# Output projection of two token blocks: seven half-size products for eight, with stored weight sums

## The chip, the core and the metric

The kernel runs on one core of a Trainium2 chip. The core has a matrix engine (TensorE: PE, with its weight loads PEld), a vector engine (DVE), a scalar engine (ACT), a general engine (POOL), and SyncE (SP), which here issues nearly all DMA transfers. The metric is the device time of one execution in microseconds; the time before is the median of three.

## The reference

Two independent branches are computed and laid side by side. Branch A is an attention with 32 heads that share one key and one value head. Branch B is a real part of a two-dimensional Fourier transform, written as products with given matrices.

```python
# A: x (2048 x 1024), wq (1024 x 1024), wk, wv (1024 x 32), wo (1024 x 1024)
q = (x @ wq).reshape(B, S, 32, 32).transpose(0, 2, 1, 3)
k = x @ wk
v = x @ wv
p = softmax(einsum("bhqd,bkd->bhqk", q, k) * 32 ** -0.5)
o = einsum("bhqk,bkd->bhqd", p, v)
out_a = o.transpose(0, 2, 1, 3).reshape(B, S, 1024) @ wo
# B: x (2048 x 1024), four transform matrices
a = einsum("bsd,ed->bse", x, hid_re); b = einsum("bsd,ed->bse", x, hid_im)
out_b = einsum("ts,bse->bte", seq_re, a) - einsum("ts,bse->bte", seq_im, b)
concatenate([out_a, out_b], axis=-1)
```

The change touches the last line of A, `o @ wo`: 2048 tokens by 1024 by 1024.

## The kernel before

**Arithmetic.** Inputs are 32-bit floats. For the projections and for branch B each operand is split into a high part, a cast to `F32R`, and a low part, what is left of it. A product of two operands is three matmuls: high x high, low x high, high x low (`product`). Each is 128 x 128 by 128 x 512. POOL casts the high part (`hi_r`, `hi_m`) and subtracts for the low part (`lo`); where an operand is a sum of blocks, POOL adds first (`comb`).

**Two streams on TensorE.** One is the attention, cut into 32 units (4 blocks of 512 tokens by 8 groups of 4 heads). A unit is 32 steps; a step has two score matmuls for row maxima and row sums of a later unit (`scores`, tiles `pss`, then a row maximum on DVE and an exponential on ACT), two score matmuls that give exponentials (`expo`, tiles `pst`), and every 8th step 32 small products with the values (`pv`, 128 x 32 weights, tiles `psb`). The main loop has 1024 steps; the row sums run 44 steps ahead (`SU + LEAD`) and so end at step 980.

The other stream is a list of groups that holds everything else: the query projection (positions 0 to 768 of the list), the first stage of branch B (768 to 2112), its second stage (2112 to 4800), then the output projection of the blocks 0 to 2 (`o_group`, 4800 to 5376). Eight more groups, the output projection of block 3, are added shortly before the end and run behind the loop, with the attention's last piece. A position is one matmul; `pos["fill"]` is where the list stands. `goal` and `level` spread the list over the steps: 404 positions lie ahead of the loop, then (5376 - 404 - 24 - 44) / 1024 = 4.789 a step, and one more a step from step 980 on. TensorE executes exactly this interleaving.

**Sevenfold products.** Both stages of branch B already go by seven half-size products in place of eight (`STAGE1`, `PRODUCTS`): sums of blocks are multiplied, and results are added up in partial sums kept in DRAM. In the first stage a group is 12 matmuls; its fifth product (name `p5`, positions 1536 to 1728) loads two partial sums for every group (`y`), adds TensorE's result on DVE and stores both.

**Output projection.** The attention's result for a unit is scaled, cast and subtracted on POOL (`ends`), and its two parts go to DRAM (`oh_d`, `ol_d`). `o_group` takes 128 tokens and 512 output columns: 8 inner blocks x 3 = 24 matmuls, one copy out of the accumulator on DVE, one store. The left parts are loaded ready split, two transfers of 256 KB for four inner blocks; `wo` is loaded and split on the way (`wo_set`, 8 tiles for 512 columns).

**What sets the order.** The program is written out by hand in order, engine by engine (`Ordered`); each engine executes its instructions strictly so. `pump` decides, as the list advances, which loads and splits are issued: an operand has a due position (`due`) and each stage of its preparation a lead (`lead`: 52, 36, 27 and 21 positions for left operands, 40, 40, 14 and 8 for right ones), and a limited number of buffers. Partial sums are loaded 24 positions ahead of the end of their group, at most `NY` = 6 at a time. Stores are issued `BEHIND` = 9 positions after the work that they wait for (`soon`, `at`). SP doesn't know positions: it runs through its list until an instruction has to wait, for a buffer, for a result, or for one of the transfers before it. A store that waits for a result therefore holds everything behind it, and what stands between two such stores goes out as soon as the first has been issued.

Of the kernel before, what the change touches and what calls it, by code (L numbers as in the profile page):

```python
# [16 lines left out]
P = 128  # L17
# [4 lines left out]
W = 512  # L22
NG = 8
NQ = 4
NC = 16
ND = D // P

# [28 lines left out]


class Ordered:

# [9 lines left out]
class Item:  # L69


    def __init__(self, srcs, save=None, pre=None, raw=None):
        self.srcs, self.save, self.pre, self.raw = srcs, save, pre, raw
        self.need = self.last = self.due = self.t = None

# [12 lines left out]
def tile_kernel(ctx: ExitStack, tc, xT, wq, wkv, wo, xbT, wT, cT, out):  # L88
# [14 lines left out]
    ql_d = [[dram.tile([P, W], F32, name=f"ql_{b}_{g}") for g in range(NG)] for b in range(NQ)]  # L103
    oh_d = [dram.tile([NG, P, W], F32, name=f"oh_{b}") for b in range(NQ)]
    ol_d = [dram.tile([NG, P, W], F32, name=f"ol_{b}") for b in range(NQ)]
    r_d = [dram.tile([NC, P], F32, name=f"r_{u}") for u in range(NQ * NG)]
# [73 lines left out]
    def load_r(it):  # L180
# [360 lines left out]
    def o_left(b, t, q):  # L541
# [5 lines left out]
        return Item(None, pre=src)  # L547

    halves = []

# [136 lines left out]
    def pv(u, k):  # L687
# [12 lines left out]
        if k == NC // 4 - 1:  # L700
            b, g = units[u]
            hi_ = onp.tile([P, W], F32R, name="oh")
            lo_ = onp.tile([P, W], F32R, name="ol")
# [184 lines left out]
```

## Time and profile before

| what | value |
|---|---|
| median of three executions | 2765.34 us (2765.29 to 2765.43) |
| profiled execution, own time | 2764.96 us |
| its span, first to last instruction | 2762.9 us |
| PE busy | 2750.9 us |
| ACT, POOL, DVE busy | 2173.0, 1650.2, 1599.3 us |
| DMA | 458.01 MB, 52.7% of 16 engines' span on SP's queue |
| TensorE's granted clock | 1.000 |

The page of a profile gives busy times, the chain of work that ended last (followed back from the last instruction), and groups of equal instructions with busy time, mean duration and the idle time just before them. Matmuls overlap: the busy time of a group counts each from start to end. A name on the left of `<-` is what is written, the one on the right what is read; `psb`, `pss` and `pst` are accumulators, `rh` and `rl` high and low part of a right operand, `mh` and `ml` of a left one, `y` a partial sum, `m` and `r` raw operands, `nm` row maxima. Since nearly every instruction is recorded by one helper, all carry its line, and groups are told apart by names. A row of a DMA queue gives packets, megabytes and the share of 16 engines' time; a row of issues ends in the median time from issue to landing. A row of waits reads: who waited, for whom, microseconds in total, times, the longest.

### The profile page before, as it was taken

The numbers are of one execution on the slowest core, as the hardware profiler recorded it, in microseconds if no ns is written. First come the engines' busy times: TensorE is split into PE (matmuls) and PEld (weight loads), VectorE is DVE, ScalarE is ACT, GpSimd is POOL, SyncE is SP. The second block draws the span as 40 slices with busy tenths as digits, with TensorE's granted clock in tenths as the row PEclk, the third lists the DMA queues.
The fourth block names the chain that finished last, engine by engine and source line by source line (L and its number), as shares of the span: only waits on it lengthen the run. The fifth ranks groups of instructions, "written<-read, shape, count | busy, mean of one in ns | idle before, by whom it ended". The sixth has DMA issues, their size and how long they took to land.

```text
span 2762.9 us, 39957 instructions
## 1 busy us (share of the span) xinstructions
PE 2750.9 (100%) x13868; PEld 1927.0 (70%) x13868; DVE 1599.3 (58%) x1830; ACT 2173.0 (79%) x3131; POOL 1650.2 (60%) x1620
## 2 busy tenths in 40 slices
PE   9999999999999999999999999999999999999999
PEld 6767676766767676676767677666676767677667
DVE  5766666666666665555555565555565555556411
ACT  3588788888888888888888888878888888888741
POOL 4845525655536447767785576798887885640110
PEclk9999999999999999999999999999999999999999
DMA  7643336765675555554463454555555552554455
GB/s 270 196 130 121 123 99 196 235 221 186 208 246 196 168 164 164 154 164 139 148 189 111 127 165 126 182 191 162 170 182 150 173 166 79 162 159 140 123 168 179
DMA packets 302473, 458.01 MB, mean 166 GB/s; under 512 B 31040, under 2 KB 96320, under 8 KB 302272
## 3 DMA queue, kind: packets, MB, share of 16 engines
q1 hardware_dynamic: 301120, 453.50, 52.7%
q8 instruction: 109, 1.79, 0.3%
q10 hardware_dynamic: 1152, 1.97, 0.2%
q14 instruction: 92, 0.75, 0.1%
HBM read 349.44 MB, written 104.60 MB: 164 GB/s over the span
## 4 chain that ended last, share of the span: by engine, by line
PE 97%; POOL 1%; DMA 1%; DVE 1%; issue 0%; ACT 0%; SPq 0%; POOLq 0%; ACTq 0%; DVEq 0%
PE psb L66 60%; PE pss L66 19%; PE pst L66 17%; POOL y L66 0%; DVE nm L66 0%; SPq L66 0%; DMA u<-y 0%; DVE y L66 0%; ACT p L66 0%; DMA p<-in_xT_dram 0%; POOL ml L66 0%; DMA m<-in_cT_dram 0%; DMA r<-s 0%; ACT pss L66 0%; POOL rl L66 0%
## 5 line engine op out<-in xcount | busy, mean ns | idle before, releaser
L66 DVE TENSOR_REDUCE nm<-pss 128x1 f32<-128x1024 f32 x1024 | 1252.5, 1223 | 576.8 <-PE pss L66 576.3
L66 ACT ACTIVATE p<-pst 128x1024 f32<-128x1024 f32 x1026 | 1052.7, 1026 | 457.9 <-PE pst L66 453.9
L66 ACT ACTIVATE pss<-pss,nm 128x1024 f32<-128x1024 f32 x1024 | 1112.3, 1086 | 63.1 <-DVE nm L66 61.1
L66 PE MATMUL psb<-rh,ml 128*128 128x512 f32 x1806 | 711.2, 394 | 3.7 <-POOL ml L66 3.7
L66 PE MATMUL psb<-rh,mh 128*128 128x512 f32 x1806 | 710.9, 394 | 0.4 <-ACT rh L66 0.4
L66 PE MATMUL psb<-rl,mh 128*128 128x512 f32 x1806 | 709.9, 393 | 0.8 <-DVE rl L66 0.8
L66 PE MATMUL pss<-kst,qst 128*128 128x512 f32 x2048 | 657.4, 402 | 0.1
L66 PE MATMUL pst<-qst,kst 128*128 128x512 f32 x2048 | 648.3, 397 | 0.9 <-ACT p L66 0.7
L66 PEld LDWEIGHTS pss<-kst,qst 128*128 128x128 f32 x2048 | 372.5, 188 | 182.9 <-issue 99.7
L66 PE MATMUL psb<-p,v 128*32 128x512 f32 x4096 | 466.0, 596 | 0.8 <-DVE y L66 0.8
L66 POOL TENSOR_TENSOR ml<-m,mh 128x512 fp32r<-128x512 f32 x338 | 436.3, 1291 | 33.8 <-ACT mh L66 26.4
L66 PEld LDWEIGHTS pst<-qst,kst 128*128 128x128 f32 x2048 | 379.4, 188 | 104.4 <-ACT p L66 16.0
L66 PEld LDWEIGHTS psb<-rh,ml 128*128 128x128 f32 x1806 | 339.4, 188 | 83.9 <-POOL ml L66 5.6
L66 PEld LDWEIGHTS psb<-rh,mh 128*128 128x128 f32 x1806 | 339.4, 188 | 82.9 <-ACT rh L66 2.1
L66 PEld LDWEIGHTS psb<-rl,mh 128*128 128x128 f32 x1806 | 339.4, 188 | 80.8 <-DVE rl L66 1.7
L66 POOL TENSOR_TENSOR r<-r,r 128x512 f32<-128x512 f32 x112 | 144.4, 1289 | 302.2 <-DMA r<-s 158.7
L66 PEld LDWEIGHTS psb<-p,v 128*32 128x32 f32 x4096 | 120.4, 110 | 276.7 <-issue 262.1
L66 POOL CAST mh<-m 128x512 fp32r<-128x512 f32 x337 | 206.4, 612 | 158.8 <-PE psb L66 141.2
L66 POOL CAST rh<-r 128x512 fp32r<-128x512 f32 x208 | 127.7, 614 | 249.9 <-PE psb L66 159.7
L66 POOL TENSOR_TENSOR rl<-r,rh 128x512 fp32r<-128x512 f32 x208 | 268.6, 1292 | 3.9
L66 POOL TENSOR_TENSOR m<-m,m 128x512 f32<-128x512 f32 x192 | 247.9, 1291 | 29.9 <-DMA m<-in_xbT_dram 21.4
L66 DVE TENSOR_TENSOR ov<-ov,psb 128x512 f32<-128x512 f32 x96 | 66.1, 688 | 288.7 <-PE psb L66 288.7
(91 smaller groups left out, 961.9 us busy)
## 6 DMA issues: line engine op xcount, KB each, us to landing
m<-in_cT_dram SPq DMA_DIRECT2D x384, 256.0 KB, 3.7
r<-s SPq DMA_DIRECT2D x192, 256.0 KB, 4.3
y<-y SPq DMA_DIRECT2D x96, 256.0 KB, 4.6
r<-in_wT_dram SPq DMA_DIRECT2D x80, 256.0 KB, 3.8
m<-in_xbT_dram SPq DMA_DIRECT2D x80, 256.0 KB, 4.1
y<-u SPq DMA_DIRECT2D x80, 256.0 KB, 2.9
m<-in_wq_dram SPq DMA_DIRECT2D x64, 256.0 KB, 3.1
qst<-qh SPq DMA_DIRECT2D x64, 256.0 KB, 5.3
```

The source lines that it names most:

```text
L66: return lambda *a, **k: self.tc.keep_in_program_order(f(*a, **k))
```

## The change

The output projection of the blocks 0 and 1 (1024 tokens, 1024 inner, 1024 columns) becomes seven half-size products (`OUTPUT`, `o_products`). Each is 512 tokens by 512 by 512, in four groups of 128 tokens (`MO`), 4 inner blocks x 3 = 12 matmuls a group. An entry names the left blocks that are added (token block, half of the inner dimension, sign), the right ones (half of the inner dimension, half of the columns, sign) and the results (token block, half of the columns, sign). They stand at positions 4800 to 5136; block 2 follows with 8 groups as before, to 5328. The list has 48 matmuls fewer, and the pace becomes (5328 - 404 - 24 - 44) / 1024 = 4.742 positions a step.

Left blocks: POOL only scales a unit of the first two blocks; the result goes to DRAM unsplit, in one transfer (`o_d`). A group loads one or two left blocks raw (256 KB each, 48 in all) and POOL adds (20 times), casts and subtracts for each group (28 times).

Right blocks: `w_parts` makes the 28 right operands (7 products x 4 tiles) early. Every 50 positions from 430 on one or two tiles of `wo` are loaded into `h2` and `h3` (48 loads), 16 positions later POOL adds, casts into `h4` and subtracts, and 12 later both parts are stored to `w_d` (56 stores). The products load them ready split (`rh`, `rl`, 56 loads), one product ahead.

Results: 12 pairs of product and result, 4 tiles each. The first for a result is copied and stored to `c_d`, each further one loads the partial sum into one of 8 tiles (`h0` to `h7`, `home`), 30 positions ahead of the end of its group, adds on DVE and stores it, at last to the output: 32 loads, 48 stores, 32 adds, 12 copies.

`spare` now has two tiles for third right operands in branch B, where it had five; `h2` to `h4` are in use.

```diff
+MO = 4
...
+OUTPUT = [
+    ([(0, 0, 1), (1, 1, 1)], [(0, 0, 1), (1, 1, 1)], [(0, 0, 1), (1, 1, 1)]),
...
-                it.t.append(spare(0, 5))
+                it.t.append(spare(0, 2))
...
     def load_y(it):
-        it.y = yp.tile([P, W], F32, name="y0")
+        if it.home:
+            turn["y"] = turn.get("y", -1) + 1
+            it.y = hp.tile([P, W], F32, name=f"h{turn['y'] % 8}")
+        else:
+            it.y = yp.tile([P, W], F32, name="y0")
...
-        while ydone[0] < min(len(ylist), yused[0] + NY) and ylist[ydone[0]].due - 24 <= pos["fill"]:
+        while ydone[0] < len(ylist) and ydone[0] < yused[0] + (8 if ylist[ydone[0]].home else NY) and ylist[ydone[0]].due - (30 if ylist[ydone[0]].home else 24) <= pos["fill"]:
...
+    def w_parts(p, step):
+        for f, (_, rt, _) in enumerate(OUTPUT):
+            for c in range(4):
+                def load(rt=rt, c=c):
+                    got.append([hp.tile([P, W], F32, name=f"h{2 + n}") for n in range(len(rt))])
+                    for t, (j, e, _) in zip(got[-1], rt):
+                        sp.dma_start(t, wo[(j * 4 + c) * P:(j * 4 + c + 1) * P, e * W:(e + 1) * W])
+                def split(rt=rt):
+                    t = got.pop(0)
+                    if len(rt) > 1:
+                        (gp.tensor_add if rt[1][2] > 0 else gp.tensor_sub)(t[0], t[0], t[1])
+                    hi, lo_ = hp.tile([P, W], F32, name="h4").bitcast(F32R), t[0].bitcast(F32R)
+                    gp.tensor_copy(hi, t[0])
+                    gp.tensor_sub(lo_, t[0], hi.bitcast(F32))
+                    made.append((hi, lo_))
+                def put(f=f, c=c):
+                    for to, of in zip(w_d[f][c], made.pop(0)):
+                        move(sp, to, of)
+                    ready.add(("w", f, c))
+                at(p, load)
+                at(p + 16, split)
+                at(p + 28, put)
+                p += step
...
+    def o_products():
...
+            R = [Item(None, pre=lambda f=f, c=c: have(("w", f, c), w_d[f][c])) for c in range(4)]
+            for k in range(MO):
+                left = [Item([(l_src(i, j, k), sg) for i, j, sg in lt])]
...
+                def post(ps, plan=plan):
+                    first = None
+                    for it, sg, to, key in plan:
+                        if it is None:
+                            if first is None:
+                                first = op.tile([P, W], F32, name="qh")
+                                dve.tensor_copy(first, ps)
+                            store(to, first, key)
+                        else:
+                            (dve.tensor_add if sg > 0 else dve.tensor_sub)(it.y, it.y, ps)
+                            store(to, it.y, key)
+                yield Group(left, R, post, ys=ys, part=([R], 0))
...
-    rest += [o_group(b, t, e, ws) for e, ws in ((1, w1), (0, w0)) for b in range(NQ - 1) for t in range(4)]
+    rest += list(o_products()) + [o_group(2, t, e, ws) for e, ws in ((1, w1), (0, w0)) for t in range(4)]
...
+            if b < 2:
+                def scaled():
+                    o = onp.tile([P, W], F32, name="oh")
+                    gp.tensor_mul(o, ov[u], rb[u])
+                    store(o_d[b][g], o, ("o", b, g))
+                ends.append(scaled)
+                return
...
+    w_parts(430, 50)
```

What this does to the order shows at three places. First SP in the first stage's fifth product. `u4` and `s` are its two results, `y0` the partial sums, `r0`, `m0` and `m1` raw operands. Before:

```order
L66 DMA u4_0_0_201<-y0_7133 128x512
L66 DMA s11_8_375<-y0_7135 128x512
L66 DMA y0_7347<-u2_1_1_218 128x512
L66 DMA y0_7349<-u3_1_1_226 128x512
L66 DMA r0_7352<-in_wT_dram 128x512
L66 DMA u4_1_0_233<-y0_7182 128x512
L66 DMA s01_8_343<-y0_7184 128x512
L66 DMA y0_7399<-u2_0_2_187 128x512
L66 DMA y0_7401<-u3_0_2_195 128x512
```

After, at the same place; `w0` and `w1` are the high and the low part of a weight sum, from `h4` and `h2`:

```order
L78 DMA u4_0_0_271<-y0_7397 128x512
L78 DMA s11_8_445<-y0_7399 128x512
L78 DMA w0_5_2_171<-h4_7530 128x512
L78 DMA w1_5_2_172<-h2_7418 128x512
L78 DMA y0_7622<-u2_1_1_288 128x512
L78 DMA y0_7624<-u3_1_1_296 128x512
L78 DMA r0_7627<-in_wT_dram 128x512
L78 DMA u4_1_0_303<-y0_7454 128x512
L78 DMA s01_8_413<-y0_7456 128x512
L78 DMA y0_7678<-u2_0_2_257 128x512
L78 DMA y0_7680<-u3_0_2_265 128x512
```

Two stores have come between the group's own stores and the next loads; elsewhere in this product loads of `wo` stand there.

Second SP in the output projection. Before, for block 1: left parts (`mh`, `ml`), a store of the output (`qh`), a tile of `wo`:

```order
L66 DMA mh_23913<-oh_1_122 128x4x128
L66 DMA ml_23914<-ol_1_126 128x4x128
L66 DMA out_0_dram<-qh_23891 128x512
L66 DMA mh_23989<-oh_1_122 128x4x128
L66 DMA ml_23990<-ol_1_126 128x4x128
L66 DMA r0_24021<-in_wo_dram 128x512
L66 DMA mh_24034<-oh_1_122 128x4x128
L66 DMA ml_24035<-ol_1_126 128x4x128
L66 DMA out_0_dram<-qh_23999 128x512
```

After, in the second product: two stores of results (`c01`, `c11`), a weight part (`rh`, `rl`), a partial sum that the product before has just stored (`h5` from `c11_1`), two raw left blocks:

```order
L78 DMA c01_1_188<-qh_24316 128x512
L78 DMA c11_1_196<-h1_24136 128x512
L78 DMA rh_24368<-w0_2_3_149 128x512
L78 DMA rl_24369<-w1_2_3_150 128x512
L78 DMA h5_24424<-c11_1_196 128x512
L78 DMA m0_24428<-o_1_122 128x4x128
L78 DMA m1_24430<-o_1_122 128x4x128
L78 DMA c01_2_189<-qh_24374 128x512
L78 DMA c11_2_197<-h2_24216 128x512
```

A group of 24 matmuls had five or six transfers. One of 12 now has seven, and a load of a partial sum stands behind the store of the same tensor.

Third DVE there. Before, one copy of an accumulator (`qh` from `psb`) for a group, between the attention's row maxima:

```order
L66 COPY qh_23764<-psb_23687 128x512
L66 TENSOR_REDUCE nm_23371<-pss_23766 128x1
L66 TENSOR_TENSOR ov_23254<-ov_23254,psb_23776 128x512
L66 TENSOR_REDUCE nm_23371<-pss_23796 128x1
L66 TENSOR_REDUCE nm_23371<-pss_23814 128x1
L66 TENSOR_REDUCE nm_23371<-pss_23839 128x1
L66 TENSOR_REDUCE nm_23371<-pss_23857 128x1
L66 TENSOR_REDUCE nm_23371<-pss_23880 128x1
L66 COPY qh_23891<-psb_23807 128x512
```

After, in the second product, a copy and an add for a group of half the length:

```order
L78 COPY qh_24316<-psb_24261 128x512
L78 TENSOR_TENSOR h1_24136<-h1_24136,psb_24261 128x512
L78 TENSOR_REDUCE nm_23518<-pss_24325 128x1
L78 TENSOR_REDUCE nm_23518<-pss_24346 128x1
L78 COPY qh_24374<-psb_24320 128x512
L78 TENSOR_TENSOR h2_24216<-h2_24216,psb_24320 128x512
L78 TENSOR_TENSOR ov_24165<-ov_24165,psb_24378 128x512
L78 TENSOR_REDUCE nm_23518<-pss_24396 128x1
L78 TENSOR_REDUCE nm_23518<-pss_24413 128x1
```

The adds (`h1`, `h2` and so on) read a partial sum that a DMA has brought; the row maxima stand behind them.

More of the change, by code (lines that the diff above doesn't have):

```diff
@@ L73, in __init__ @@
         self.srcs, self.save, self.pre, self.raw = srcs, save, pre, raw
-        self.need = self.last = self.due = self.t = None
+        self.need = self.last = self.due = self.t = self.home = None
 class Group:
@@ new lines, in tile_kernel, with l_src, src @@
+    got, made = [], []
+    def o_products():
+        seen = {}
+        total = {(i, e): sum((i, e) == o[:2] for p in OUTPUT for o in p[2]) for i in range(2) for e in range(2)}
+        for f, (lt, rt, outs) in enumerate(OUTPUT):
+            def l_src(i, j, k):
+                b, t = divmod(i * MO + k, 4)
+                def src():
+                    assert all(("o", b, g) in ready for g in range(4 * j, 4 * j + 4)), (b, t, j)
+                    return o_d[b][4 * j:4 * j + 4, :, t * P:(t + 1) * P].rearrange("g p c -> p g c")
+                return src
+            R = [Item(None, pre=lambda f=f, c=c: have(("w", f, c), w_d[f][c])) for c in range(4)]
+            for k in range(MO):
+                left = [Item([(l_src(i, j, k), sg) for i, j, sg in lt])]
+                ys, plan = [], []
+                for i, e, sg in outs:
+                    n = seen.get((i, e, k), 0)
+                    seen[i, e, k] = n + 1
+                    it = None
+                    if n:
+                        it = Item([(lambda i=i, e=e, k=k, n=n: have(("c", i, e, k, n), c_d[i, e][k]), 1)])
+                        it.home = True
+                        ys.append(it)
+                    r0 = (i * MO + k) * P
+                    end_ = n + 1 == total[i, e]
+                    plan.append((it, sg, out[r0:r0 + P, e * W:(e + 1) * W] if end_ else c_d[i, e][k], None if end_ else ("c", i, e, k, n + 1)))
+                def post(ps, plan=plan):
[10 more added lines that the diff above has]
+                yield Group(left, R, post, ys=ys, part=([R], 0))
```

9 lines of the change are left out of this document (6 added, 3 removed), and 6 rows, old and new, of the table OUTPUT.

## The prediction, made before the result was known

> **What bounds the kernel now.** I read the page first (busy time, chain, groups), then TensorE's rows in order of time, then stages, DMA, and the waits of SP.
>
> ```profile
> PE 2750.9 (100%) x13868; PEld 1927.0 (70%) x13868; DVE 1599.3 (58%) x1830; ACT 2173.0 (79%) x3131; POOL 1650.2 (60%) x1620
> ...
> PE 97%; POOL 1%; DMA 1%; DVE 1%; issue 0%; ACT 0%; SPq 0%; POOLq 0%; ACTq 0%; DVEq 0%
> ...
> L66 PE MATMUL psb<-rh,ml 128*128 128x512 f32 x1806 | 711.2, 394 | 3.7 <-POOL ml L66 3.7
> ```
>
> TensorE is the bound: 2750.9 of 2762.9 us, and 97% of the chain that ended last. So a matmul taken away is worth time, if operands still arrive in time. It isn't worth the 394 ns of its group, since neighbours overlap. What it is worth is the distance between starts:
>
> ```profile
> 40.07 0.40 PE L66 MATMUL psb<-rh,mh 128*128 128x512 f32 x1
> ...
> 44.62 0.40 PE L66 MATMUL psb<-rh,ml 128*128 128x512 f32 x1
> ...
> 1500.90 0.40 PE L66 MATMUL psb<-rh,ml 128*128 128x512 f32 x1
> ...
> 1502.05 0.62 PE L66 MATMUL pss<-kst,qst 128*128 128x512 f32 x2
> ```
>
> From 40.07 to 44.62 are 20 starts, 228 ns each; from 1500.90 to 1502.05, among scores, five, 230 ns each. I take 230.
>
> **Removed matmuls.** Two blocks of tokens cost 8 row tiles x 2 column halves x 24 = 384 matmuls; seven products cost 7 x 4 x 12 = 336. That is 48 fewer: 48 x 0.230 = 11.0 us, shared over the run, since the pacing rule spreads the list over 1024 steps: 4.789 list matmuls a step before, 4.742 after. By the Trainium skill, "TensorE: Matmul & The Clock Gate", section "Wait — 56ns, not 53.3ns?", a warm matmul of 512 columns starts every 215.7 ns, which would make it an estimated 10.4 us; the rows here show 228 to 230, so the measurement decides.
>
> **Where the products run.** The chain's groups of 32 matmuls are the value products, one every 8 steps (steps 8, 976, 984 and 1016):
>
> ```profile
> 155.76 3.57 PE psb L66 x32
> ...
> 2595.11 3.57 PE psb L66 x32
> 2613.92 3.57 PE psb L66 x32
> ...
> 2687.74 4.73 PE psb L66 x37
> ```
>
> A step takes (2595.11 - 155.76) / 968 = 2.520 us, after the change 2.520 - 0.047 x 0.230 = 2.509; from step 980, without scores, (2687.74 - 2613.92) / 32 = 2.31. List position 4800, where the products begin, is step (4800 - 404) / 4.742 = 927, at 155.76 + 919 x 2.509 = 2461 us; position 5136, their end, is step 995, at 2629 us. So 168 us. A group of 12 list matmuls lasts 6.3 us in the five first products and 4.8 us in the last two (5.74 list matmuls a step).
>
> **Added work of the engines in those 168 us.**
>
> ```profile
> L66 DVE TENSOR_REDUCE nm<-pss 128x1 f32<-128x1024 f32 x1024 | 1252.5, 1223 | 576.8 <-PE pss L66 576.3
> ...
> L66 POOL TENSOR_TENSOR ml<-m,mh 128x512 fp32r<-128x512 f32 x338 | 436.3, 1291 | 33.8 <-ACT mh L66 26.4
> ...
> L66 POOL CAST rh<-r 128x512 fp32r<-128x512 f32 x208 | 127.7, 614 | 249.9 <-PE psb L66 159.7
> ...
> L66 DVE TENSOR_TENSOR y<-y,psb 128x512 f32<-128x512 f32 x112 | 75.0, 682 | 18.4 <-PE psb L66 17.5 <-DMA r<-in_wT_dram 0.6 <-DMA u<-y 0.2
> ...
> 600.00:900.00 300.00, 299.57 (x1526) 207.83 (x1526) 197.03 (x228) 249.29 (x359) 157.22 (x152) 1.00 0.64 209
> ...
> 2434.00:2595.00 161.00, 161.00 (x822) 112.19 (x820) 94.13 (x106) 134.25 (x196) 32.55 (x32) 1.00 0.49 144
> 2595.00:2700.00 105.00, 104.90 (x544) 69.29 (x543) 17.94 (x31) 50.70 (x56) 13.15 (x15) 1.00 0.51 154
> ```
>
> POOL: 28 left blocks x (614 + 1291) + 20 sums x 1291 = 79 us. The stage rows (their columns: PE, weight loads, DVE, ACT, POOL, clock, DMA share, GB/s) give it 32.55 us of 161 and 13.15 of 105, so with the 79 about 65% of 168 us. Densest is the last product: 4 left blocks and the third block's 8 weight tiles, 12 x 1.9 = 22.8 us in 19; but the last tile's low part stands 29 list matmuls (11 us) ahead of its use. Covered. DVE: 32 adds and 12 copies at about 0.69 = 30 us for 11 us of evacuations; in the worst product two per 6.3 us, beside 2.5 row maxima of 1.22: 1.4 + 3.1 + about 0.6 for the rest = 5.1 of 6.3 us. Covered, if no add waits for its partial sum. If that cover goes, row maxima stand behind the waiting add, then ACT's exponentials, then the score banks, and TensorE is late within two steps.
>
> Weight sums, positions 430 to 1808: 28 x (614 + 1291) + 20 x 1291 = 79 us of POOL in about 730 us, a burst of 1.9 or 3.2 us every 50 positions (26 us). POOL is busy 157.22 of 300 us there: covered. POOL saves a cast and a subtraction for each of the 16 units of the two blocks, 16 x 1.9 = 30 us, which were covered too: zero. A third right operand has two buffers for five (`spare`), but the second operand's two (`r1`) hold the line to two loads ahead already: zero.
>
> **DMA and SP's queue, where I see the risk.** In the section: 48 loads of left blocks, 56 of weight parts, 32 loads and 48 stores of partial results, 184 of 256 KB, 48.2 MB in 168 us: 287 GB/s for the 144 of the row above. Outside: 48 loads and 56 stores for the weight sums, less 16 stores of low parts. The nearest rows for a full queue (10 to 30 us; 728 to 832, the first stage's fifth product; 2440 to 2600):
>
> ```profile
> q1 hardware_dynamic: 4270, 7.77, 104.8%
> ...
> h<-in_xT_dram SPq DMA_DIRECT2D x8, 256.0 KB, 5.4
> ...
> q1 hardware_dynamic: 13906, 25.01, 76.1%
> ...
> y<-u SPq DMA_DIRECT2D x32, 256.0 KB, 2.7
> u<-y SPq DMA_DIRECT2D x17, 256.0 KB, 3.9
> ...
> q1 hardware_dynamic: 31620, 21.71, 45.3%
> ```
>
> Pure loads reached 7.77 MB / 20 us = 389 GB/s. Mixed traffic at a share of one would be 25.01 / 104 / 0.761 = 316, or 21.71 / 160 / 0.453 = 300 GB/s. 287 is 91 to 96% of the mixed rates, 74% of the pure one. Local peaks go over: the sixth product has 29 transfers in 8 steps x 2.31 = 19 us, 7.6 MB, 25 us at 300 GB/s, 6 us too many. What hides that is lead: SP runs ahead of TensorE to the next store that waits for a result, so a partial sum is asked for some 40 list matmuls early (16 us), weight parts at least 29 (12 us), left blocks over 50 (20 us). A lag of 6 to 10 us on landings of 4 to 5 us is about spent there. The Trainium skill, "DMA: Bandwidth & Descriptors", section "Measured (HBM→SBUF, 128 partitions, SWDGE, issued from GpSimd)", asks for batches of 1 MiB and fits 2.0 us + bytes / 436 GB/s, an estimated 2.6 us for each of these if nothing overlapped, 478 us in all. The 10 to 30 us row speaks against that: the same size overlapped to 389 GB/s.
>
> SP is the other limit. The fifth product of the first stage has the same shape (two loaded partial sums, two stores, per 12 matmuls), and there SP goes like this:
>
> ```profile
> 764.94 0.84 SPq L66 DMA_DIRECT2D y<-u  x2
> 765.87 0.86 SPq L66 DMA_DIRECT2D m<-in_xbT_dram  x2
> 766.78 0.42 SPq L66 DMA_DIRECT2D u<-y  x1
> 767.25 0.43 SPq L66 DMA_DIRECT2D s<-y  x1
> 771.71 0.94 SPq L66 DMA_DIRECT2D y<-u  x2
> ...
> SPq L66 <- DMA u<-y: 36.1, 13, 4.5
> SPq L66 <- DVE y L66: 16.8, 15, 7.3
> ...
> PE psb L66 <- POOL ml L66: 3.7, 4, 1.2
> ...
> PE psb L66 <- DVE y L66: 0.8, 2, 0.5
> ```
>
> An issue costs 0.43 us; after its stores SP stood 4 us for their landing before the next loads. In that product (104 us) it waited 36.1 us for such landings and 16.8 us for DVE, which is its slack, and TensorE lost 0.8 us to DVE in the whole run. The weight sums add 13 transfers there: 13 x 0.43 = 5.6 us of SP, 13 x 0.262 / 316 = 11 us of DMA (share 0.76 to 0.87). The 5.6 fit into the 16.8; most stores stand where SP waits anyway. Bounds: 0 (the slack takes it) and 11 us (each adds its transfer time); nearer to 0: 1 us.
>
> In the section a group issues two stores, waits for their landing, then one partial sum and two left blocks: 0.43 + 3.9 + 3 x 0.43 = 5.6 us of 6.3, with 0.5 for the units' own transfers; 4.8 us groups with such a wait are only the four of the sixth product. Bounds: 0, and 24 us (third rival). I take 1.5 us, since the leads cover the first 12 us.
>
> **Sum.** 2764.96 (the profiled execution, 0.38 under the median) - 11.0 + 1 + 1.5 = 2756.5, and 2757 against the median.
>
> **Rivals.**
> 1. The weight sums make the first stage's partial sums late: the 11 us above, paid on TensorE's path. 2765.3 - 11 + 11 + 1 = 2766, no change. For it: 36.1 us of landing waits. Against it: 0.8 us lost so far.
> 2. POOL's bursts and the new phase lengthen its waits: the 3.7 us row doubles. 2757 + 3.7 = 2761. Against it: its 3.7 us fall in the second stage, where nothing is added and the list goes 0.4% slower.
> 3. Slower: in the section every partial sum waits on SP for a store that is landing. At the full queue's 5.4 us a group needs 0.43 + 5.4 + 1.3 + 0.5 = 7.6 us. The 16 groups of the products with such a wait in the slow part lose 1.3 each, the four quick ones 2.8: 32 us, of which the leads absorb at most 12. With 4 us for left blocks and weights late: 24 us, 2765.3 - 11 + 24 = 2778. It decides when stores land later than about 4.1 us, where 5.6 + 0.5 us reaches 6.3. The row of 3.9 us, at a share of 0.76, is just under that. The Trainium skill, same page, section "Latency and other measured facts", gives HBM access 0.2 us on average and 2 us at high load, which speaks for this rival; the trace agrees in kind (loads 2.7 us at 0.76, 5.4 us on the full queue).
> 4. Each matmul is worth its 394 ns: 48 x 0.394 = 18.9, 2747. The starts speak against it.
>
> **Chances.** Forecast (2754 to 2760) 0.52, rival 1 0.14, rival 2 0.10, rival 3 0.21, rival 4 0.03. 0.2% is 5.5 us, about what a measurement of this kernel can tell from no change: faster is the forecast, half of rival 2 and rival 4, 0.60; the same is rival 1 and the other half, 0.19; slower is rival 3, 0.21. The range goes from 2753.5 (nothing paid, and up to a microsecond of POOL's waits saved) to 2770, which leaves out most of rival 3.
>
> **What would show it.** Right: 48 fewer list matmuls at 228 to 230 ns, steps of 2.51 us, a DMA share near 0.9 from 2461 to 2629 us with TensorE still full, DVE waits for loads under 2 us. Rival 1: TensorE idle between 720 and 840 us, released by DVE's adds, and less of SP's wait on DVE. Rival 3: TensorE idle after 2480 us, released by DVE, by the weight parts or by left blocks, with stores landing over 5 us. I am wrong if the section's share reaches one for tens of microseconds.

## The result and the profile after

The changed kernel takes 2770.64 us (median of 14 executions, 2767.85 to 2774.39), the kernel before beside it 2765.35 us (14 executions, 2764.07 to 2767.23). The ratio is 1.0019, 95% interval 1.0011 to 1.0028: slower by 5.3 us, where 2757 was forecast. The profiled execution of the changed kernel took 2772.16 us, 1.5 above its median.

The page of the changed kernel, the lines that answer to those of before:

```profile
PE 2748.9 (99%) x13820; PEld 1917.4 (69%) x13820; DVE 1616.2 (58%) x1858; ACT 2172.0 (78%) x3131; POOL 1778.1 (64%) x1740
...
q1 hardware_dynamic: 322624, 503.85, 58.3%
...
PE 93%; DMA 2%; POOL 1%; ACT 1%; DVE 1%; issue 1%; SPq 1%; POOLq 0%; ACTq 0%; DVEq 0%
...
L78 PE MATMUL psb<-rh,ml 128*128 128x512 f32 x1790 | 705.7, 394 | 7.0 <-POOL ml L78 5.8
L78 PE MATMUL psb<-rh,mh 128*128 128x512 f32 x1790 | 705.5, 394 | 4.4 <-DMA mh<-oh 3.4
```

The 48 matmuls are gone (13868 to 13820), but TensorE's busy time fell by 2.0 us only, the span grew by 7.5, and 4 of the 97% of the chain that ended last went from TensorE to transfers, ACT, SP and others. POOL's `ml` now costs TensorE 5.8 us instead of 3.7, and a load that had cost nothing, `mh<-oh` (left parts of block 2's projection), 3.4 us.

Where it happened is read from the value products, one group of 32 matmuls every 8 steps, since both kernels have the same 1024 steps. Their rows in TensorE's timeline (start, duration, xcount), of before at steps 664, 680, 976 and 1000:

```profile
1808.65 3.64 PE L66 MATMUL psb<-p,v 128*32 128x512 f32 x32
1851.27 3.64 PE L66 MATMUL psb<-p,v 128*32 128x512 f32 x32
2595.04 3.64 PE L66 MATMUL psb<-p,v 128*32 128x512 f32 x32
2650.83 3.64 PE L66 MATMUL psb<-p,v 128*32 128x512 f32 x32
```

and of the changed kernel at the same steps:

```profile
1804.01 3.64 PE L78 MATMUL psb<-p,v 128*32 128x512 f32 x32
1851.94 4.30 PE L78 MATMUL psb<-p,v 128*32 128x512 f32 x32
2593.49 3.64 PE L78 MATMUL psb<-p,v 128*32 128x512 f32 x32
2657.82 4.13 PE L78 MATMUL psb<-p,v 128*32 128x512 f32 x32
```

Eleven microseconds over 1024 steps are 0.0108 us a step. Against that:

| steps | lead of the changed kernel at the end | change in this stretch | forecast | lost |
|---|---|---|---|---|
| 0 to 664 | 4.6 us ahead | -4.6 | -7.1 | 2.5 |
| 664 to 680 | 0.7 us behind | +5.3 | -0.2 | 5.5 |
| 680 to 976 | 1.5 us ahead | -2.2 | -3.2 | 1.0 |
| 976 to 1000 | 7.0 us behind | +8.5 | -0.3 | 8.8 |
| 1000 to 1024 | 7.4 us behind | +0.4 | -0.3 | 0.7 |

Two stretches hold 14.3 of the 18.5 us lost: 42 us in branch B's second stage, where the change adds nothing, and some 60 us around the last two of the seven products, after step 980, where the list runs faster. The stages before (columns: PE, weight loads, DVE, ACT, POOL with their counts, granted clock, DMA share, GB/s):

```profile
1780.00:1860.00 80.00, 76.31 (x390) 51.87 (x389) 43.48 (x50) 62.93 (x91) 70.76 (x66) 1.00 0.64 198
...
2605.00:2665.00 60.00, 60.00 (x306) 40.83 (x305) 8.13 (x20) 28.27 (x30) 3.20 (x3) 1.00 0.49 151
```

and after:

```profile
1780.00:1860.00 80.00, 72.64 (x363) 47.67 (x363) 39.60 (x47) 56.62 (x83) 70.28 (x66) 0.96 0.67 203
2434.00:2605.00 171.00, 170.90 (x874) 118.89 (x867) 109.91 (x129) 141.38 (x206) 93.41 (x91) 1.00 0.84 261
2605.00:2665.00 60.00, 53.70 (x263) 32.81 (x262) 13.78 (x29) 22.98 (x25) 32.05 (x35) 0.97 0.88 277
```

The slow part of the section (2434 to 2605 us) is full, at a DMA share of 0.84. In both bad stretches TensorE is idle and its granted clock falls.

**The first stretch.** POOL is at its limit there in both kernels: before, it works for 70.76 of 80 us and waits for raw right operands (`r<-s`) for 9.1 more; after, for 70.28 and 8.0. In time order, the changed kernel's POOL, and the matmul that waits for it:

```profile
1837.10 1.29 POOL L78 TENSOR_TENSOR ov<-ov,rb 128x512 f32<-128x512 f32 x1
...
1840.83 0.61 POOL L78 CAST oh<-ov 128x512 fp32r<-128x512 f32 x1
...
1844.46 1.27 POOL L78 TENSOR_TENSOR m<-m,m 128x512 f32<-128x512 f32 x1
1845.69 1.27 POOL L78 TENSOR_TENSOR ol<-ov,oh 128x512 fp32r<-128x512 f32 x1
1846.91 1.27 POOL L78 TENSOR_TENSOR ml<-m,mh 128x512 fp32r<-128x512 f32 x1
...
1848.23 0.79 PE L78 MATMUL psb<-rh,ml 128*128 128x512 f32 x1 [3.65 <-POOL ml L78]
```

and before:

```profile
1842.39 1.30 POOL L66 TENSOR_TENSOR ov<-ov,rb 128x512 f32<-128x512 f32 x1
...
1845.59 1.27 POOL L66 TENSOR_TENSOR ml<-m,mh 128x512 fp32r<-128x512 f32 x1
1846.79 0.61 POOL L66 CAST oh<-ov 128x512 fp32r<-128x512 f32 x1
...
1846.91 0.50 PE L66 MATMUL psb<-rh,ml 128*128 128x512 f32 x1 [1.22 <-POOL ml L66]
```

A unit's end (`ov`, `oh`, `ol`, 3.2 us on POOL) comes with the attention's steps, the left parts with the list. The new pace moved the one against the other: now all three instructions stand ahead of the `ml` that TensorE needs; before, only the first did. The wait grew from 1.22 to 3.65 us, and the clock followed. Windows of the changed kernel, granted clock in the third column from the end:

```profile
1848.00:1850.00 2.00, 1.77 (x4) 1.48 (x5) 0.00 (x0) 0.00 (x0) 2.00 (x4) 0.50 0.30 79
1850.00:1852.00 2.00, 2.00 (x9) 1.05 (x12) 1.22 (x1) 0.81 (x1) 2.00 (x2) 0.50 0.94 311
1852.00:1854.00 2.00, 2.00 (x17) 0.53 (x20) 0.00 (x0) 1.32 (x3) 2.00 (x3) 0.67 1.05 393
```

and of before:

```profile
1846.00:1850.00 4.00, 3.09 (x13) 2.55 (x14) 1.65 (x2) 2.54 (x4) 4.00 (x6) 1.00 0.50 139
```

2.4 us more of waiting and some 5 us at half speed, which cost about 2.5: nearly all of the 5.5 us. That is the price in this execution. The six kernels made for the second stretch, below, have the same instructions in this stage; in their traces the wait is 3.61 to 3.64 us, the clock is low for 3.4 us, and steps 664 to 680 cost 3.5 to 4.6 us of lead, against 5.3 here.

**The second stretch.** The chain of waits of the changed kernel, its three longest links there (start, duration), a tile of block 2's weights and two left parts:

```profile
2621.41 5.24 DMA r<-in_wo_dram
...
2641.14 6.58 DMA ml<-ol
...
2650.65 4.48 DMA ml<-ol
```

Block 2's left parts were asked for late, and landed after TensorE wanted them. Ahead of these links the chain also passes two landings of stored partial sums (`c<-h`, 3.9 us at 2599.0 and 4.5 us at 2604.3). Whether SP was late because of the amount of transfers, or because of waits behind its own stores, the trace of this kernel alone doesn't tell.

### The profile page after: what moved, and what is told of

Same layout as the page of the kernel before. It is cut to its first block, busy times and chain, and to the rows that moved or that the text cites. A ratio compares the mean times of both kernels' runs of the same rounds, so it can differ in the third digit from the quotient of the medians.

```text
span 2770.4 us, 40341 instructions
## 1 busy us (share of the span) xinstructions
PE 2748.9 (99%) x13820; PEld 1917.4 (69%) x13820; DVE 1616.2 (58%) x1858; ACT 2172.0 (78%) x3131; POOL 1778.1 (64%) x1740
## 4 chain that ended last, share of the span: by engine, by line
PE 93%; DMA 2%; POOL 1%; ACT 1%; DVE 1%; issue 1%; SPq 1%; POOLq 0%; ACTq 0%; DVEq 0%
PE psb L78 58%; PE pss L78 18%; PE pst L78 17%; DMA r<-s 1%; SPq L78 1%; ACT pss L78 1%; DVE nm L78 1%; ACT p L78 0%; DMA ml<-ol 0%; DMA s<-y 0%; POOL ml L78 0%; DMA c<-h 0%; DMA r<-in_wo_dram 0%; DVE y L78 0%; POOL rl L78 0%
## 5 line engine op out<-in xcount | busy, mean ns | idle before, releaser
L78 POOL TENSOR_TENSOR ml<-m,mh 128x512 fp32r<-128x512 f32 x366 | 473.0, 1292 | 36.4 <-PE pss L78 26.4
L78 POOL CAST mh<-m 128x512 fp32r<-128x512 f32 x365 | 223.9, 613 | 167.0 <-PE psb L78 146.3
L78 POOL TENSOR_TENSOR m<-m,m 128x512 f32<-128x512 f32 x212 | 273.9, 1292 | 69.6 <-DMA m<-o 30.9
```

The costliest lines, as they stand in the source:

```text
L78: return lambda *a, **k: self.tc.keep_in_program_order(f(*a, **k))
```

## The experiments

### The weight sums alone

The kernel before, with the weight sums made and stored as in the change and read by nobody (`w_parts` as in the diff).

```diff
-                it.t.append(spare(0, 5))
+                it.t.append(spare(0, 2))
...
+    w_parts(430, 50)
```

> The kernel before with the early weight sums added (48 loads, 79 us of POOL, 56 stores, two tiles for third right operands); nothing reads them and the output projection is as before. Rival 1 of the prediction (the fifth product of the first stage starves): up to 11 us more, 2777, with TensorE waiting for DVE between 720 and 840 us. My theory now: the old phase keeps room for them, at most 1 us more, 2765 to 2767.

2765.16 us beside 2765.82; ratio 0.9997 (0.9988 to 1.0007). The 104 transfers and POOL's 28 bursts cost nothing that can be measured: the first rival's 11 us fall. The 1 us of the forecast lies inside the interval (-3.3 to +1.9 us), so this run doesn't decide it.

The profiled execution, the slowest of the ten (2766.93 us), has a stall of its own in the second stage, at the old pace:

```profile
1802.91 0.80 PE L77 MATMUL psb<-rh,ml 128*128 128x512 f32 x1 [2.27 <-POOL ml L77]
```

POOL had waited 6.4 us for a raw right operand (4.9 in the kernel before), TensorE waited 1.60 and 2.27 us, and the granted clock was 0.50 for 6.8 us. The kernel fell 4.4 us back between steps 600 and 664 and had 2.4 of it again by step 680. So that stage can stall at the old pace too, where a load is late; on average it cost nothing here.

### The first stretch: four runs

**POOL relieved of one addition.** Of the second stage's two additions into partial sums, one goes to DVE.

```diff
-                                (gp.tensor_add if sg > 0 else gp.tensor_sub)(it.y, it.y, h)
+                                eng = gp if plan[0][1] is it else dve
+                                (eng.tensor_add if sg > 0 else eng.tensor_sub)(it.y, it.y, h)
```

> The changed kernel, and in the second stage the second of a group's two additions to partial sums runs on DVE in place of POOL. Theory P: the stall near 1790 to 1850 us is POOL's order and amount of work in one product (two left sums, two additions, a right tile and a unit's end fill its 12.6 us a group), so 1.3 us less for a group removes it. TensorE's waits for POOL's low parts fall from 5.8 us to under 1, the clock is 1.00 throughout, and the time falls by the 3.7 us that before lost there too and the 5.8 more of now: 2761. Rival: POOL is late because its own loads come late under the larger traffic; then at least 5 us of waits stay and the time is 2766 to 2771.

2773.3 us, ratio 1.0025 (1.0015 to 1.0034). A miss: the stretch from step 672 to 680 lost 5.3 us again, and TensorE still waited 4.6 us for `ml`. One of two additions that stood shortly ahead of the `ml` in question was gone, but POOL waited for raw right operands instead of working (`r<-s`, 13.8 us from 1780 to 1860 us, 8.0 in the changed kernel). Less work alone doesn't bring `ml` earlier, and the late loads of the expectation's rival may have a part in it.

**The old pace up to step 912.** The list goes at 4.789 a step until step 912, and at 4.37 after it, so that the section of seven products has the same number of matmuls spread thinner.

```diff
+    TURNS = 912
...
-        return PRO + (FILL - PRO - LAST - MORE * (total - QUIET)) * n // total + MORE * max(n - QUIET, 0)
+        old = PRO + (FILL + 48 - PRO - LAST - MORE * (total - QUIET)) * n // total
+        if n <= TURNS:
+            return old
...
+        return at_ + (FILL - LAST - MORE * (total - QUIET) - at_) * (n - TURNS) // (total - TURNS) + MORE * max(n - QUIET, 0)
```

> The changed kernel with the pace of before (4.789 list matmuls a step) up to step 912 and 4.37 from there, so that until position 4771 every list matmul meets the same step as before. Theory P in its narrow form: the stall near 1800 us grew because a unit's end now falls in front of a needed low part; with the old phase it costs 3.7 us as before and not 9.5: 2765. Rival: the added weight sums and transfers made it grow; then it stays at 9.5 us and the time at 2770.

2761.53 us, ratio 0.9981 (0.9972 to 0.9991), 3.5 us under the expected 2765. Up to step 912 this kernel stays 1.1 to 1.3 us behind the one before (2.0 at step 664 alone), without growth, and its longest wait for `ml` is 1.5 us: with the old phase the stall is the old one. The section itself gained 4.2 us of the 11. ACT's exponentials (2.31 us a step in all) began to hold the score matmuls, whose steps had become 2.42 us long; by the distances between starts that took some 3 us up to step 976, an estimate. From step 976 to 1000 only 0.8 us of lead went, where the changed kernel lost 8.5. So the gain of this run isn't the first stretch's alone.

**The unit ends on DVE, in the changed kernel and in the one before.**

```diff
-            e = dve if last else gp
+            e = dve
```

> The changed kernel with the three instructions at a unit's end (scale, cast, low part) of the blocks 2 and 3 on DVE in place of POOL. Theory P in its narrow form: near 1850 us a unit's end (3.2 us of POOL) stands in front of the low part that TensorE waits for; without it that wait of 3.7 us and the half-speed clock behind it go: 5 to 9 us less, 2762 to 2766. Rival: POOL waits for right tiles that come late, whatever stands behind them; then under 2 us are won: 2769 or more.

> The kernel before with the unit ends of all blocks on DVE in place of POOL, nothing else: what that edit is worth without the change. In the trace of the kernel before POOL's waits of that stage cost TensorE 3.7 us and the granted clock stayed at 1.00 there, so about 2765.5 - 3.5 = 2762, 2760 to 2764. Rival (the edit is worth the same 8 to 9 us in any kernel, so that what it gave to the changed kernel says nothing about the change): 2757. Other rival (DVE is late with the products' copies when it has the unit ends as well): 2765 or more.

In the kernel before this moves the unit ends of all four blocks, in the changed one those of the blocks 2 and 3, the only ones that still have three instructions. The units that end in the first stretch are of block 2 in both.

The changed kernel: 2761.56 us, ratio 0.9988 (0.9979 to 0.9997), 9.1 us below the change as it was. Its row for the first stretch:

```profile
1780.00:1860.00 80.00, 80.00 (x411) 55.86 (x410) 49.23 (x56) 67.52 (x98) 71.92 (x67) 1.00 0.67 209
```

No idle time, no lowered clock, POOL as busy as ever. Between steps 976 and 1000 it lost 6.8 us all the same: the second stretch is another matter. The kernel before: 2765.98 us, ratio 1.0000 (0.9991 to 1.0008). There the expectation of 2762 missed: its waits for `ml` fell from 3.7 to 1.0 us, but the span from 2762.9 to 2762.5 only: by step 368, ahead of the second stage, it had fallen 1.6 us back, and why stays open. The comparison that counts is by stretch. From step 600 to 680 the edit gains 3.1 us in the kernel before and 9.3 in the changed one; so some 6 us of that stall belong to the change, by its phase.

### The second stretch: six runs

**The products placed ahead of the second stage's last product**, away from the quick steps.

```diff
-    rest += list(stage1()) + list(stage2())
+    two = list(stage2())
+    rest += list(stage1()) + two[:-16] + list(o_products()) + two[-16:]
...
```

> The changed kernel with the seven products ahead of the last product of the second stage, at positions 4416 to 4752, where every group of 12 still lasts 6.3 us. Theory Q: the 7 us lost between steps 992 and 1000 come from the amount of transfers where the list goes quickly (products six and seven, the weight tiles of block 2); moved away, they are not lost: 2763, and TensorE waits neither for DMA nor for POOL in the new section. Rival R: each group's load of a partial sum behind its own store is too slow on SP anywhere; then 5 us or more are lost in the new place too: 2769 to 2772. A third: the last product of the second stage, now in the quick part, runs out of POOL and loses as much: 2770.

2786.77 us, ratio 1.0074 (1.0059 to 1.0089). A confounded experiment: the right operands of the product that now follows, 8 sums of two blocks, came due within 48 positions instead of 192. TensorE waited for POOL:

```profile
PE psb L78 <- POOL ml L78: 22.2, 5, 9.1
```

Of the 22.2 us, 3.6 are the first stretch's; two waits of 9.1 and 8.0 us, with the clock at 0.50 behind them, make the loss of 25.6 us between steps 912 and 920. What it still shows is that, with the products moved away from the quick steps, nothing is lost between steps 976 and 1000 (23.6 us behind, then 23.2).

**No partial sums loaded.** The 32 loads and additions are left out, and with them the sums.

```diff
-                    if n:
-                        it = Item([(lambda i=i, e=e, k=k, n=n: have(("c", i, e, k, n), c_d[i, e][k]), 1)])
-                        it.home = True
-                        ys.append(it)
```

> The changed kernel without the 32 loads and additions of partial sums in the output projection: every product's result is copied and stored alone, so results of the blocks 0 and 1 are not summed up. Theory Q (amount of transfers in the quick part): 152 in place of 184 transfers and no load behind its own store; the 7 us between steps 992 and 1000 fall to under 2: 2765. Rival S: the loss is the chain of the weight tiles of block 2 (load, POOL, buffer, next load, with the left parts behind it on SP); then 5 us or more stay there: 2769.

2759.71 us, ratio 0.9979 (0.9969 to 0.9988): the loss after step 976 is gone. This leaves two causes: 32 transfers fewer, or no load behind a store.

**Weights of block 2 loaded earlier**, four of its tiles of `wo` ahead of the last product's right operands.

```diff
+    early = w1[:4]
...
+    RL.items[at7:at7] = early
+    for c, it in enumerate(early):
+        it.due = made7[-MO].at - 72 + 9 * c
...
```

> The changed kernel with the first four of block 2's eight weight tiles ahead of the last product's right operands in the line, so that the eight are spread over some 110 list positions in place of 48. Nothing less is transferred. Theory S: the loss between steps 992 and 1000 is the crowd of these tiles (load, POOL, buffer, next load) with the left parts behind it on SP; it falls from 7 us to under 2: 2765. Theory Q: the amount of transfers in the two last products decides; then 4 us or more stay: 2768 or more.

2770.4 us, ratio 1.0016 (1.0007 to 1.0026). A miss: 7.3 us are lost from step 984 to 992 all the same, with TensorE now waiting 4.8 us for stored weight parts (`rh<-w`). Moving loads about in the queue moves the place where it is late, not the lateness.

**As many loads, but of old tiles.** The 32 loads read tiles of the same size that were stored long before, so that the sums are of other data; transfers, additions and stores are all there.

```diff
-                        it = Item([(lambda i=i, e=e, k=k, n=n: have(("c", i, e, k, n), c_d[i, e][k]), 1)])
+                        it = Item([(lambda i=i, e=e, k=k: s_d[i, e][k], 1)])
```

> The changed kernel whose 32 loads of partial sums read tiles of the first stage, long complete, in place of the partial sums just stored; as many transfers and additions, but no load waits for its store, and the sums are of other data. Theory R (SP stands behind its own store): the section loses what it lost without the loads altogether: 2761. Theory Q (amount of transfers): as slow as the changed kernel in the quick part: 2769 to 2771.

2762.25 us, ratio 0.9986 (0.9977 to 0.9995), 8.4 us below the change. Not all of that is the loads': of the 9.9 us between the two profiled executions 3.5 were there by step 904, where both kernels still run the same instructions. From step 976 to 1000 the changed kernel lost 8.5 us of lead and this one 2.0. So the amount isn't the cause by itself; the waiting behind the own store is most of it. SP's timeline in the changed kernel, at the first loads for the sixth product and at the first load for block 2 (`c` is a partial sum in DRAM, `h` its tile):

```profile
2584.00 0.33 SPq L78 DMA_DIRECT2D c<-h  x1
2584.66 0.33 SPq L78 DMA_DIRECT2D rh<-w  x1
2585.23 0.32 SPq L78 DMA_DIRECT2D rl<-w  x1
2589.58 0.80 SPq L78 DMA_DIRECT2D h<-c  x2
...
2635.28 1.65 SPq L78 DMA_DIRECT2D h<-c  x2
2637.02 0.38 SPq L78 DMA_DIRECT2D mh<-oh  x1
```

and in the kernel that loads old tiles (`s`):

```profile
2578.72 0.33 SPq L78 DMA_DIRECT2D c<-h  x1
...
2579.93 0.41 SPq L78 DMA_DIRECT2D rl<-w  x1
2580.39 0.97 SPq L78 DMA_DIRECT2D h<-s  x2
...
2626.17 0.90 SPq L78 DMA_DIRECT2D h<-s  x2
2627.16 0.38 SPq L78 DMA_DIRECT2D mh<-oh  x1
```

TensorE is 3.5 us earlier in the second kernel (value product of step 984 at 2609.91 and 2613.45). SP is 5.3 us earlier at the first of these rows, 9.2 at the load, 9.9 at `mh<-oh`. So its lateness against TensorE grew from 1.8 to 5.7 us at one load that stood behind a landing store, and was 6.4 when block 2's left parts were asked for. SP's waits for landing stores in the changed kernel, first from 2475 to 2560 us and then from 2560 to 2640 us (total, times, longest):

```profile
SPq L78 <- DMA c<-h: 13.5, 7, 3.0
SPq L78 <- DMA c<-qh: 9.6, 4, 3.0
...
SPq L78 <- DMA c<-h: 13.4, 6, 3.7
```

The stores that they wait for land so late (issues between 2461 and 2629 us; the last column is the median time to landing):

```profile
c<-qh SPq DMA_DIRECT2D x16, 256.0 KB, 4.7
c<-h SPq DMA_DIRECT2D x15, 256.0 KB, 4.4
```

In the stretch up to 2560 us SP stood 23 us for stores, and TensorE was full: the leads held. But the slack was gone: there the kernel with old tiles had SP wait 7.6 us for results from DVE (`h`, `qh`), a sign that it was ahead of TensorE, and the changed kernel 0.3. In the stretch after it the kernel with old tiles has 4.5 us of waits for stores:

```profile
SPq L78 <- DMA c<-h: 4.5, 5, 2.1
```

And from the first to the last `h` row above, seven groups apart, SP takes 6.5 us a group in both kernels ((2635.28 - 2589.58) / 7 and (2626.17 - 2580.39) / 7), while TensorE takes 6.3 up to step 980 and 4.8 behind it, by the steps some 5.4 on average here. From the first `h` row to `mh<-oh`, some 48 us, SP's issues take 26 in either kernel. The rest is waiting: in the changed kernel 10.5 us for stores and 7.4 for POOL, which splits block 2's weight tiles, in the other 4.5 and 5.7. So SP loses lead in the quick groups with or without the loads of fresh partial sums; the 6 us of lateness that the changed kernel brought into them then came through.

**Another order of the seven products**: rows 1, 2, 5, 4, 6, 3, 7 of the table. As it was, five of the six neighbouring pairs share a quarter of the result; now only the first does. The sixth place, in the quick steps, also goes to a product with one result instead of two, 4 loads and 4 stores fewer there, so this run doesn't tell the order from the amount; the load of old tiles does.

```diff
-    ([(1, 0, 1), (0, 0, -1)], [(0, 0, 1), (0, 1, 1)], [(1, 1, 1)]),
-    ([(1, 0, 1), (1, 1, 1)], [(0, 0, 1)], [(1, 0, 1), (1, 1, -1)]),
     ([(0, 1, 1), (1, 1, -1)], [(1, 0, 1), (1, 1, 1)], [(0, 0, 1)]),
+    ([(1, 0, 1), (1, 1, 1)], [(0, 0, 1)], [(1, 0, 1), (1, 1, -1)]),
     ([(0, 0, 1), (0, 1, 1)], [(1, 1, 1)], [(0, 0, -1), (0, 1, 1)]),
+    ([(1, 0, 1), (0, 0, -1)], [(0, 0, 1), (0, 1, 1)], [(1, 1, 1)]),
     ([(1, 1, 1)], [(1, 0, 1), (0, 0, -1)], [(0, 0, 1), (1, 0, 1)]),
```

> The changed kernel with the seven products in another order: rows 1, 2, 5, 4, 6, 3, 7 of its table, everything else as it was. As it stood, five of the six neighbouring pairs share a quarter of the result, so that a partial sum is loaded 4 groups of 12 matmuls after the group that stored it; now only the first pair does, in the slow part. Transfers, their number and POOL's and DVE's work are the same. Theory R (SP stands behind its own landing store wherever a partial sum was just written): the loss of 7 to 9 us between steps 976 and 1000 goes, the growth of the POOL stall at 1790 to 1850 us stays: about 2762, 2760 to 2764. Rival (any load of a partial sum next to stores costs it; that the neighbours share a quarter is chance): 2769 to 2772. If the order moves the peak of weight loads instead, something between, with another place of the loss.

2764.84 us, ratio 0.9997 (0.9988 to 1.0005). Half a hit: 5.8 us better than the change, 2.8 short of the expectation; 4.4 us of lead were still lost between steps 976 and 1000.

**The new order, and the last but one unit's end on DVE.**

```diff
-            e = dve if last else gp
+            e = dve if u + 2 >= len(units) else gp
```

> The products in the order 1, 2, 5, 4, 6, 3, 7, and of the unit ends only that of the last but one unit moved from POOL to DVE. In the run with the new order alone 4.4 us were still lost between steps 976 and 1000, and in its trace this unit's three POOL instructions stand at 2641.66 to 2646.55 us, in the middle of it, with two stores on SP behind them; with all unit ends on DVE nothing is lost there. Theory U (that one unit end makes the rest of the quick part's loss): the loss between these steps is under 1.5 us, the stall at 1790 to 1850 us stays as it was, so about 2761, 2759 to 2763. Rival (the rest of the loss comes from the earlier stall, or from the units before, and this one is chance): 4 us are lost there again, 2764 to 2767.

2763.03 us, ratio 0.9990 (0.9981 to 0.9999), at the upper end of what was expected. In its trace the loss between steps 976 and 1000 is 0.3 us, as that theory says, and the stretch is full:

```profile
2605.00:2665.00 60.00, 59.72 (x302) 39.31 (x301) 14.14 (x27) 26.89 (x27) 32.53 (x35) 1.00 0.96 297
```

The medians, though, differ by 1.8 us from the run with the order alone, not by the 4.1 us of the traces (their ranges are 2760.83 to 2765.78 and 2762.36 to 2767.03, and the two profiled executions lie near opposite ends). So that unit end has a part in it; how large it is on average these runs don't settle.

### Both mended

The new order of the products and all unit ends on DVE.

> Both mendings together: the products in the order 1, 2, 5, 4, 6, 3, 7 and the unit ends of blocks 2 and 3 on DVE in place of POOL. If the two losses are separate causes at separate places (POOL at 1790 to 1850 us, SP at 2605 to 2660 us), their gains add: 2770.4 - 8.6 - 8.5 = about 2753.5, 2751 to 2756, 0.43% under the kernel before, and the ten to eleven microseconds of the forecast's matmuls are there whole. Rival (one limit behind both, or a next one close behind, such as DVE in the last steps): no better than the better of the two alone, 2760 to 2762.

2757.98 us, ratio 0.9971 (0.9961 to 0.9982), the fastest of all kernels here, though 2 us above the expected range. Both stretches are full:

```profile
1780.00:1860.00 80.00, 79.73 (x405) 54.83 (x405) 50.38 (x55) 66.20 (x97) 70.36 (x65) 1.00 0.67 212
...
2605.00:2665.00 60.00, 59.73 (x313) 38.44 (x315) 12.86 (x20) 26.69 (x26) 33.14 (x36) 1.00 0.87 272
```

The two losses are two causes, and their mendings add, nearly: of 2770.64 us the ends alone take 9.1, the order alone 5.8, both 12.7. (The runs are of different chips; the kernel before took 2765.35, 2765.82 and 2766.18 us beside them.) Against the kernel before with its unit ends on DVE (2765.98 us, same chip) the seven products are worth 8.0 us.

## Why the prediction was wrong

- **48 x 0.230 = 11.0 us: right.** With the unit ends on DVE on both sides the changed kernel leads by 11.1 us at step 912 (value products at 2423.72 and 2434.81), where the term gives 9.8; the kernel with both mended, which differs up to there only in the order of the weight sums, leads by 8.4. The gain was there and was given back.
- **1 us for the first stage's fifth product: too small to be seen** in the run with the weight sums alone. The changed kernel did lose 2.5 us by step 664; 2.0 of it were there by step 368, and no run attributes them.
- **"Where nothing is added": the first failed step.** The second rival was put at 3.7 us and one in ten, and its counterargument was that the second stage gets no new work and a list 0.4% slower. It named the right place and the wrong quantity. POOL's load is the same before and after; what changed is which of its instructions stands ahead of `ml`. A pace that differs by 1% had moved the list by 664 x 0.047 = 31 matmuls against the units, one group of 24 and 7 more. The mechanism is shown by the old pace (no growth) and the moved unit ends (no stall); that a late load can stall the same stage at the old pace is seen in one execution of the weight sums alone. Its price was 5.5 us in the profiled execution, since the wait of 3.65 us also brought the clock to 0.50; the rival had doubled a sum of four short waits.
- **1.5 us for the section, "since the leads cover the first 12 us": the step that failed most.** The third rival's mechanism was true, and its condition was met: the stores of partial sums landed after 4.4 (`c<-h`) and 4.7 us (`c<-qh`) in the median, over the 4.1 from which it was to decide, though not the 5 us that it named as its sign. Its place was not the slow part. There the rival had every group stand for a whole landing and fall 1.3 us short of TensorE, 21 us in 16 groups. SP stood 23 us from 2475 to 2560 us, under 2 us for each of some 13 groups and never over 3.0 at once, so part of each landing was over when SP came to wait; TensorE lost 1.0 us from step 680 to 976. What failed is the count of the quick groups, "only the four of the sixth product", and the 12 us of lead set against them. SP took 6.5 us a group for seven groups there where TensorE takes 4.8, because of its issues, the stores and POOL's weight tiles together. So the lead was spent whether SP waited for fresh partial sums or not, and the lateness from those waits came through: 8.8 us instead of 1.5. That this is near the 4 x 2.8 = 11.2 us of the rival's quick groups is in part luck, since that sum has neither the weight tiles nor the lowered clock.
- **DMA rates: right.** 287 GB/s were forecast for 2461 to 2629 us; the trace has 274 at a share of 0.87, and the share was not the limit, as the load of old tiles shows with as many transfers.

```profile
2461.00:2629.00 168.00, 167.10 (x845) 115.89 (x844) 102.07 (x126) 131.79 (x186) 91.15 (x89) 1.00 0.87 274
```

- By terms: -11.0, 5.5 in the second stage instead of 0, 8.8 in the section instead of 1.5, 4.2 in other places instead of 1, together +7.5 in the profiled pair and +5.3 in the medians. With both causes mended the kernel takes 2758 us, near the 2757 of the forecast, but that is another kernel.

## What to carry to other kernels

A change of the pace between two interleaved streams is a change everywhere, since it shifts which instruction of one stream stands ahead of the other's on a busy engine: look for engines near 90% in every stage, not only where work is added. In an in-order DMA queue a load of what was just stored holds all transfers behind it until the store has landed (3.7 us at one load here), so order the work so that a result is read back several groups later. And book a lead as an account: subtract what each stage of a section draws from it before it is used to cover the next.

## What the runs showed of the hardware

In the traces the granted clock is low for 3.41 us or a multiple of it. In the changed kernel one wait of TensorE of 3.65 us brought it to 0.50 for 6.83 us, beginning while TensorE still waited; in six other kernels the same wait, 3.61 to 3.64 us, brought it down for 3.41. So the wait cost an estimated 1.7 to 2.5 us more than itself. Shorter waits close together did the same: 2.09 and 1.05 us between 2651 and 2656 us of the changed kernel, and 1.60 and 2.27 in the kernel before with the weight sums. Single waits of up to 1.76 us left the clock at 1.00 (with the unit ends on DVE, 1.72 and 1.76). The Trainium skill, "TensorE: Matmul & The Clock Gate", section "What's actually happening", says that the clock falls to half after one idle window of about 3.4 us and returns after one that is busy. The traces agree on the length, but here it fell without a whole idle window: in the 3.41 us ahead of the first low stretch of the changed kernel TensorE was idle for 1.9.

The changed kernel's executions spread over 6.5 us, those of the kernel before over 3.2, and those with both causes mended over 2.4 (8 executions). The first stall alone doesn't explain that: with the unit ends on DVE, and that stall gone, the changed kernel spreads over 7.3 us. No run tested the reason.
